# Sparse attention and a split-precision MLP on one core: weights in sixteen 1 MB blocks, and the round trip on ScalarE's queue

## The chip, the cores and the metric

The kernel runs on one core of a Trainium2 chip. A core has TensorE (PE, with its weight load PEld), VectorE (DVE), ScalarE (ACT), GpSimd (POOL) and SyncE (SP), a data memory SBUF of 128 partitions, an accumulation memory PSUM, and 16 DMA engines. The metric is device microseconds for one execution. "Granted clock" is the share of TensorE's full clock that it was given.

## The reference

```python
# q, k, v: (8, 8, 576, 64); x: (8, 576, 512)
scores = q @ k.T / 8                      # heads 0-3: causal, the last 32 positions
scores = where(mask, scores, -1e9)        # heads 4-7: causal, same position modulo 32
attn_out = softmax(scores) @ v            # heads side by side: x
h = (x.T @ U @ V).T                       # rank 32, over the sequence
u = x + h
out = u + max(u @ w_ch1, 0) @ w_ch2       # w_ch1 (512, 2048), w_ch2 (2048, 512)
```

q, k and v are float32. U, V and the two weights are float64: each number reaches the chip as a 64-bit word and is made into a float32 there.

## The kernel before, in words

**The GEMM.** The 8 x 576 rows of u are 36 tiles of 128 rows, 18 blocks of two. Each block n goes through 16 steps (n, fc). A step has a first GEMM (`gemm1`, L521: 12 matmuls of 128x256 into PSUM tile `ph`, for 128 of the 2048 hidden columns), then on ScalarE `gh` (relu, rounded to the short format fp32r, L525) and on VectorE `gl` (the rest that the rounding lost, L526), and two steps later a second GEMM (`gemm2`, L538: 6 matmuls of 128x512 into `acc`). Three matmuls per product give float32 accuracy: `uh`, `ul` and the two halves of a weight tile `w` are the rounded part and the rest. `ph` has two buffers, so the first GEMM of a step waits for gl of two steps earlier. Blocks 0 and 1 run interleaved (32 steps, block 1 two fc behind), then 2 to 17 in order.

**The weights.** 32 chunks of 128x512: four of w1 and four of w2 for every four steps. Each is loaded as 64-bit words (`raw`, 512 KB, L138, issued on SP behind the last other transfer traced) and converted by `to_f32`: ScalarE takes the absolute value of the high word (L104), a clamp at 2^-15 runs on GpSimd, for every third chunk on VectorE (L105), and VectorE makes the exponent, the sign and the low bits (L107, L109, L111). ScalarE rounds it into `w` (L150), GpSimd subtracts to get the rest (L151). The tile being made is `cv`, one of six buffers of tag "att" that the attention shares.

**Attention.** `attention_pair` and `local_pairs` do two heads: scores on TensorE (L215, L221) into `px`, maximum and subtraction on VectorE (L230, L231), exp on ScalarE, transposes (L241), outputs (L253), and the norm on VectorE (L263 to L265, six operations, result `o_sb` or `xg`). Batches 0 and 1 do all eight heads this way; heads 4 to 7 come out in another row order, so their result is written to DRAM (`od`) and read back into `xg` and `xt`: the round trip, L199 to L208, on SP's queue like every transfer. Batches 2 to 7 do those heads on GpSimd and VectorE (`strided_heads`).

**Mix.** `mix_t` (L373, L377; sums `ta`, then `tst`) and `mix_u` (L399, L401) add h. `transposes` (L486) turns u and splits it into `uh` (L490) and `ul` (L491).

**Order.** The program is written as generators that hand out the attention, the conversions and the loads step by step; `convert` and `load_ahead` say how many by when. Batch 0's attention, its mix and the first split come before the first GEMM, batch 1's attention goes between the first 32 steps. A scheduler then sets each engine's order, and an engine runs its list strictly in it. Pair buffers (`qkv`) are three: batch 0's fourth pair waits for the first to be done.

Of the kernel before, what the change touches and what calls it, by code (L numbers as in the profile page):

```python
# [39 lines left out]
def fused_kernel(ctx, tc, pairs, strided, U, V, w1_in, w2_in, masks, eye, out):  # L40
# [57 lines left out]
    def to_f32(raw, p, n, eng=nc.vector):  # L98

        rv = raw.bitcast(I32).rearrange("p (n two) -> p n two", two=2)  # L100
        lo_w, hi_w = rv[:, 0:n, 0], rv[:, 0:n, 1]
# [2 lines left out]
        nc.scalar.activation(out=f, in_=hi_w.bitcast(F32), func=AF.Abs)  # L104
        eng.tensor_scalar(out=f, in0=f, scalar1=TINY, scalar2=None, op0=ALU.max)  # L105
# [1 line left out]
        nc.vector.tensor_scalar(out=i, in0=i, scalar1=3, scalar2=0x3FFFFFF8,  # L107
                                op0=ALU.logical_shift_left, op1=ALU.bitwise_and)
        nc.vector.scalar_tensor_tensor(out=i, in0=hi_w, scalar=-0x40000000, in1=i,  # L109
# [31 lines left out]
    def weights():
        for n, (i, g, t) in enumerate(chunks):
            while wl["n"] <= n:
                next(wl["gen"])
                wl["n"] += 1
# [561 lines left out]
```

## Time and profile before

| | us |
|---|---|
| median of three runs | 1013.37 (1013.08 to 1013.67) |
| profiled execution | 1013.35 |
| its span | 1011.6 |
| PE busy | 940.6 (93%) |
| DVE busy | 608.2 (60%) |
| POOL busy | 391.3 (39%) |
| ACT busy | 267.0 (26%) |
| mean granted clock | 0.96 |

What lies outside the span (1.75 us) is start and end of the execution. Busy time is summed over the whole span, and the early part differs from the rest, so a stretch has to be looked at by itself. PE's ends are modelled: its price for a step is read from the starts of matmuls that follow each other. DMA issues are rows of SPq; the time to landing counts from the issue.

### The profile page before, as it was taken

Reading aid. Unit: us, or ns where it says so; the run is one execution under the profiler, and the core shown is the slowest. Engines: PE = TensorE matmul, PEld = TensorE weight load, DVE = VectorE, ACT = ScalarE, POOL = GpSimd, SP = SyncE. Lnnn points to the kernel's source line nnn. Section 1 sums busy time; section 2 is a strip of 40 time slices with the busy share of each in tenths; the row PEclk is TensorE's granted clock in tenths of the full one; section 3 lists DMA queues with packets and bytes.
Section 4 is the critical chain, followed back from the end, with each engine's and each line's share of the span. In section 5 each row is a group of like instructions: output and inputs, shape, how many; then the busy total and the mean of one; then the engine's idle time right before and its main releaser. Section 6 shows DMA issues by size and latency. Waiting matters only on the chain.

```text
span 1011.6 us, 20383 instructions
## 1 busy us (share of the span) xinstructions
PE 940.6 (93%) x8524; PEld 809.6 (80%) x8524; DVE 608.2 (60%) x1115; ACT 267.0 (26%) x616; POOL 391.3 (39%) x388
## 2 busy tenths in 40 slices
PE   3324999999999999999999999999999999999997
PEld 2213888888888888898888888888888889999996
DVE  4759958886974667514698368847884753212121
ACT  3334433124212421112421142114211421111110
POOL 0647536963951456302385047515661400000000
PEclk8556999999999999999999999999999999999999
DMA  9990141022111221101211121111211001101000
GB/s 358 409 300 1 62 130 48 3 85 96 69 45 42 85 80 45 42 1 43 96 68 45 43 95 70 46 43 58 106 46 43 1 22 22 42 1 43 1 21 21
DMA packets 41037, 72.74 MB, mean 72 GB/s; under 512 B 6224, under 2 KB 25552, under 8 KB 40176
## 3 DMA queue, kind: packets, MB, share of 16 engines
q1 hardware_dynamic: 40944, 71.43, 21.5%
q8 instruction: 67, 1.10, 0.5%
q14 instruction: 26, 0.21, 0.1%
HBM read 52.92 MB, written 10.62 MB: 63 GB/s over the span
## 4 chain that ended last, share of the span: by engine, by line
PE 87%; DVE 7%; DMA 3%; issue 1%; POOL 1%; ACT 0%; SPq 0%; DVEq 0%; ACTq 0%; POOLq 0%
PE ph L521 41%; PE acc L538 38%; DVE cv L109 2%; PE px L538 2%; PE px L221 2%; DVE cv L111 1%; PE px L253 1%; DVE cv L107 1%; PE px L241 1%; DMA xg<-in_U_dram 1%; PE px L373 1%; DMA xg<-od 1%; DMA od<-o_sb 1%; PE px L399 1%; POOL cv L105 0%
## 5 line engine op out<-in xcount | busy, mean ns | idle before, releaser
L521 PE MATMUL ph<-uh,w 128*128 128x256 f32 x2304 | 470.4, 287 | 4.8 <-DVE gl L526 4.1
L521 PEld LDWEIGHTS ph<-uh,w 128*128 128x128 f32 x2304 | 375.5, 189 | 21.2 <-DVE gl L526 4.2
L538 PE MATMUL acc<-w,gh 128*128 128x512 f32 x1088 | 348.0, 399 | 0.0
L521 PE MATMUL ph<-ul,w 128*128 128x256 f32 x1152 | 326.2, 283 | 3.2 <-DVE ul L491 3.2
L526 DVE SCALAR_TENSOR_TENSOR gl<-ph,gh 128x256 fp32r<-128x256 f32 x288 | 121.6, 422 | 291.2 <-ACT gh L525 289.8
L525 ACT ACTIVATE gh<-ph 128x256 fp32r<-128x256 f32 x288 | 110.5, 384 | 518.3 <-PE ph L521 480.8
L335 POOL TENSOR_TENSOR tmp<-st,s_st 128x448 f32<-128x448 f32 (+7 forms) x162 | 137.7, 878 | 276.6 <-DVE st L337 212.0
L521 PEld LDWEIGHTS ph<-ul,w 128*128 128x128 f32 x1152 | 218.4, 190 | 13.6 <-DVE ul L491 3.6
L538 PEld LDWEIGHTS acc<-w,gh 128*128 128x128 f32 x1088 | 193.1, 188 | 32.4 <-issue 0.2
L538 PE MATMUL acc<-w,gl 128*128 128x512 f32 x544 | 215.8, 397 | 0.0
L307 POOL TENSOR_TENSOR tmp<-st 128x576 f32<-128x576 f32 (+6 forms) x162 | 169.4, 1087 | 44.5 <-DVE st L337 34.3
L337 DVE TENSOR_REDUCE st<-tmp 128x64 f32<-128x64 f32 (+8 forms) x162 | 135.3, 874 | 2.8 <-POOL tmp L335 2.5
L538 PEld LDWEIGHTS acc<-w,gl 128*128 128x128 f32 x544 | 102.3, 188 | 20.9
L309 DVE TENSOR_REDUCE s_st<-tmp 128x9 f32<-128x576 f32 (+6 forms) x162 | 86.7, 564 | 5.2 <-POOL tmp L307 5.0
L151 POOL TENSOR_TENSOR w<-cv,w 128x512 fp32r<-128x512 f32 x32 | 46.7, 1468 | 44.7 <-ACT w L150 44.3
L105 POOL TENSOR_SCALAR cv<-cv 128x512 f32<-128x512 f32 x22 | 36.0, 1645 | 45.9 <-ACT cv L104 45.9
L352 ACT COPY xg<-st 32x256 f32<-32x256 f32 x96 | 38.8, 404 | 16.9 <-DVE st L337 14.8
L221 PEld LDWEIGHTS px<-qkv 64*32 64x32 f32 x1440 | 19.7, 112 | 19.8 <-issue 14.6
L508 DVE TENSOR_TENSOR ul<-u,uh 128x1024 fp32r<-128x1024 f32 x15 | 19.0, 1269 | 24.5 <-ACT uh L507 24.5
L221 PE MATMUL px<-qkv 64*32 64x64 f32 (+1 forms) x1440 | 29.5, 236 | 3.5 <-DMA qkv<-in_pairs_dram 2.0
L150 ACT CAST w<-cv 128x512 fp32r<-128x512 f32 x32 | 19.9, 621 | 45.0 <-DVE cv L111 38.3
L384 DVE TENSOR_TENSOR ta<-px,ta 32x256 f32<-32x256 f32 x42 | 17.6, 420 | 21.5 <-ACT ta L382 20.4
(90 smaller groups left out, 559.7 us busy)
## 6 DMA issues: line engine op xcount, KB each, us to landing
raw<-in_w_dram SPq DMA_DIRECT2D x32, 512.0 KB, 10.3
qkv<-in_pairs_dram SPq DMA_DIRECT2D x20, 585.0 KB, 5.5
qkv<-in_pairs_dram SPq DMA_DIRECT2D x20, 576.0 KB, 4.0
out_dram<-xg SPq DMA_DIRECT2D x32, 256.0 KB, 2.1
u<-bt SPq DMA_DIRECT2D x240, 32.0 KB, 1.9
st<-in_strided_dram SPq DMA_DIRECT2D x6, 1152.0 KB, 6.4
st<-in_strided_dram SPq DMA_DIRECT2D x6, 576.0 KB, 4.0
od<-o_sb SPq DMA_DIRECT2D x4, 256.0 KB, 7.1
```

What stands on the lines that cost most here:

```text
L105: eng.tensor_scalar(out=f, in0=f, scalar1=TINY, scalar2=None, op0=ALU.max)
L151: nc.gpsimd.tensor_tensor(out=lo, in0=f, in1=hi.bitcast(F32), op=ALU.subtract)
L221: nc.tensor.matmul(sp[32 * c4:32 * c4 + 32, hh, x0:64 * t + 64], qT[rows, 32 * c:32 * c + 32], kT[rows, k0:32 * c + 32], start=False, stop ...
L307: nc.gpsimd.tensor_tensor(out=tmp[:, 0:n], in0=sk[:, j0:j0 + n], in1=sq[:, i:i + 1].broadcast_to([128, n, D]), op=ALU.mult)
L309: late.append(lambda tmp=tmp, n=n, i=i, j0=j0: nc.vector.tensor_reduce(out=s_st[:, i, j0:j0 + n], in_=tmp[:, 0:n], axis=AX.X, op=ALU.add))
L335: nc.gpsimd.tensor_tensor(out=tv, in0=sv[:, 0:i + 1, d0:d0 + step], in1=s_st[:, i, 0:i + 1].broadcast_to([128, i + 1, step]), op=ALU.mult)
L337: late.append(lambda tv=tv, i=i, d0=d0, step=step: nc.vector.tensor_reduce(out=o_st[:, i, d0:d0 + step], in_=tv.rearrange("p j d -> p d j" ...
L352: nc.scalar.copy(out=xg[32 * i4:32 * i4 + 32, :, cs], in_=o_st[rows, i4:16:4, :])
L521: nc.tensor.matmul(ph[:, 0:W], w_parts[0, g, dc][:, part, fs], ut[:, :, :, dc, :], start=(dc == 0 and i == 0), stop=(dc == NDC - 1 and i = ...
L525: nc.scalar.activation(out=gh[:, 0:W], in_=ph[:, 0:W], func=AF.Relu)
L526: nc.vector.scalar_tensor_tensor(out=gl[:, 0:W], in0=ph[:, 0:W], scalar=0.0, in1=gh[:, 0:W].bitcast(F32), op0=ALU.max, op1=ALU.subtract)
L538: nc.tensor.matmul(accs[n][:, s, :], gt[:, cs], w_parts[1, g, f][:, part, :], start=(fc == 0 and i == 0), stop=(fc == NFC - 1 and i == 2))
```

## The change

**Weights in blocks.** On the host w1 and w2 are laid out as 16 blocks of 128 rows by 1024 words (1 MB): block fc holds what step fc needs of both. Three blocks load freely. Block fc from 3 on is held by a one-column GpSimd copy (L144) that reads block fc - 3's finished tile, so it loads when that conversion is over.

**Conversion.** There is no clamp: ScalarE copies the high word times 2^-112 (L115), VectorE shifts (L117) and puts in sign and low bits (L118, L120), for every half block. The scratch is `cv` (two buffers of its own) and `spare`, parts of the tiles of the last blocks' weights, which also hold batch 0's fourth pair and its attention's temporaries (`ring`); so the fourth pair loads at once, and "att" has four buffers. The first four blocks are converted during batch 0's attention; each later one is queued, on ScalarE and VectorE, behind the first split of u (`marks["split0"]`).

**Round trip.** All transfers from `o_sb` to `od` and back are issued by ScalarE (L97) and not by SP.

```diff
+    def od_dma(out, in_):
+        nc.scalar.dma_start(out=out, in_=in_)
...
-        nc.scalar.activation(out=f, in_=hi_w.bitcast(F32), func=AF.Abs)
-        eng.tensor_scalar(out=f, in0=f, scalar1=TINY, scalar2=None, op0=ALU.max)
+        nc.scalar.activation(out=f, in_=hi_w.bitcast(F32), func=AF.Copy, scale=2.0 ** -112)
...
-        nc.vector.tensor_scalar(out=i, in0=i, scalar1=3, scalar2=0x3FFFFFF8,
-                                op0=ALU.logical_shift_left, op1=ALU.bitwise_and)
-        nc.vector.scalar_tensor_tensor(out=i, in0=hi_w, scalar=-0x40000000, in1=i,
+        nc.vector.tensor_scalar(out=i, in0=i, scalar1=3, scalar2=None, op0=ALU.logical_shift_left)
+        nc.vector.scalar_tensor_tensor(out=i, in0=hi_w, scalar=-0x80000000, in1=i,
...
+        for fc in range(NFC):
+            raw = raws[fc] = const.tile([128, 1024], I64, name=f"w{fc}", tag=f"w{fc}")
+            if fc >= AHEAD:
+                done = w_parts[fc - AHEAD].bitcast(F32)
+                nc.gpsimd.tensor_copy(out=raw.bitcast(F32)[:, 0:1], in_=done[:, 1, 1, 0:1])
+            nc.sync.dma_start(out=raw, in_=w_in[128 * fc:128 * fc + 128, :])
             yield
 
     def weights():
+        for fc in range(NFC):
+            load_ahead(fc + 1)
+            fs = []
+            for i in range(2):
+                early = i and fc < NFC - AHEAD - 2
+                cv = late_part[fc % 2][:, 1536:2048] if early else ap_.tile([128, 512], F32, name="cv", tag="cv", bufs=2)
+                behind = [marks[k][2] for k in ("less", "exp")] if fc < PRE else marks["split0"]
+                with tc.issue_after(behind[0]), tc.issue_after(behind[1]):
+                    fs.append(to_f32(raws[fc][:, 512 * i:512 * i + 512], cv, 128, 512))
+                if not i:
+                    yield
+            parts = w_parts[fc] = const.tile([128, 2, 2, 512], F32R, name=f"w{fc}", tag=f"w{fc}")
+            for i in range(2):
+                nc.scalar.copy(out=parts[:, i, 0], in_=fs[i])
+                nc.gpsimd.tensor_tensor(out=parts[:, i, 1], in0=fs[i], in1=parts[:, i, 0].bitcast(F32), op=ALU.subtract)
+            load_ahead(fc + 1 + AHEAD)
+            yield
...
-        dma(out=od[0:512, oc:oc + 2 * D].rearrange("(t p) d -> p t d", p=128), in_=o_sb[:, 0:4, :])
-        dma(out=od[512:576, oc:oc + 2 * D], in_=o_sb[0:64, 4, :])
+        od_dma(out=od[0:512, oc:oc + 2 * D].rearrange("(t p) d -> p t d", p=128), in_=o_sb[:, 0:4, :])
+        od_dma(out=od[512:576, oc:oc + 2 * D], in_=o_sb[0:64, 4, :])
...
-        return len(chunks) if item[0] >= NLEAD else 8 * (item[1] // FPG) + 4 + item[1] % FPG
+        return 2 * NFC if item[0] >= NLEAD else 2 * item[1] + 2
```

The rows below are the engines' lists; numbers in names tell buffers apart. First, SP's list before, at batch 0's round trip (od, then xg and xt):

```order
L138 DMA raw0_2_2_474<-in_w1_dram 128x512
L138 DMA raw0_2_3_476<-in_w1_dram 128x512
L88 DMA qkv_882<-in_pairs_dram 128x1152
L88 DMA qkv_882<-in_pairs_dram 128x1170
L88 DMA od_84<-o_sb_465 128x4x128
L88 DMA od_84<-o_sb_465 64x128
L88 DMA qkv_962<-in_pairs_dram 128x1152
L88 DMA qkv_962<-in_pairs_dram 128x1170
L88 DMA qkv_1137<-in_pairs_dram 128x1152
L88 DMA qkv_1137<-in_pairs_dram 128x1170
L88 DMA xg_480<-od_84 32x4x256 x4
L88 DMA xt_481<-od_84 32x256 x2
```

The same place now, on ScalarE's list (w3 is block 3, ring_85 the o_sb of the second class pair, PT copies of the attention are L264):

```order
L115 ACTIVATE cv_589<-w3_414 128x512
L115 ACTIVATE spare_103<-w3_414 128x512
L97 DMA od_84<-ring_85 128x4x128
L97 DMA od_84<-ring_85 64x128
L264 COPY ring_86<-px_471 128x576
L162 CAST w3_606<-cv_589 128x512
L162 CAST w3_606<-spare_103 128x512
L97 DMA xg_426<-od_84 32x4x256 x4
L97 DMA xt_427<-od_84 32x256 x2
```

The trip left SP's list, where weights and batch 1's pairs stood ahead of it, and now stands on ScalarE between the steps of block 3's conversion. Second, VectorE before, in the first GEMM steps (about 120 to 127 us; six gl stand ahead of these rows):

```order
L526 SCALAR_TENSOR_TENSOR gl_1208<-ph_1194,gh_1207 128x256
L109 SCALAR_TENSOR_TENSOR cv_1126<-raw1_2_2_553,cv_1126 128x512
L107 TENSOR_SCALAR cv_1211<-cv_1211 128x512
L111 SCALAR_TENSOR_TENSOR cv_1126<-raw1_2_2_553,cv_1126 128x512
L230 TENSOR_REDUCE mx_1258<-px_1148 128x10
L109 SCALAR_TENSOR_TENSOR cv_1211<-raw1_2_3_555,cv_1211 128x512
L231 TENSOR_TENSOR s_sb_1257<-px_1148,mx_1258 128x2x5x64
L111 SCALAR_TENSOR_TENSOR cv_1211<-raw1_2_3_555,cv_1211 128x512
L526 SCALAR_TENSOR_TENSOR gl_1302<-ph_1288,gh_1301 128x256
L526 SCALAR_TENSOR_TENSOR gl_1430<-ph_1416,gh_1429 128x256
```

And VectorE now, at the end of its conversions (w15 is the last block; gl_1696, gl_1727 and gl_1766 are those of the 17th, 18th and 19th step):

```order
L551 SCALAR_TENSOR_TENSOR gl_1696<-ph_1682,gh_1695 128x256
L117 TENSOR_SCALAR cv_1699<-cv_1699 128x512
L551 SCALAR_TENSOR_TENSOR gl_1727<-ph_1713,gh_1726 128x256
L118 SCALAR_TENSOR_TENSOR cv_1699<-w15_1539,cv_1699 128x512
L117 TENSOR_SCALAR cv_1730<-cv_1730 128x512
L120 SCALAR_TENSOR_TENSOR cv_1699<-w15_1539,cv_1699 128x512
L283 TENSOR_SCALAR rt_1394<-px_1357 128x2x4
L118 SCALAR_TENSOR_TENSOR cv_1730<-w15_1539,cv_1730 128x512
L284 RECIPROCAL rt_1394<-rt_1394 128x2x4
L120 SCALAR_TENSOR_TENSOR cv_1730<-w15_1539,cv_1730 128x512
L285 TENSOR_TENSOR xg_1140<-px_1357,rt_1394 128x2x4x64
L283 TENSOR_SCALAR rt_1394<-px_1357 64x2
```

Before, the conversions thin out after the eighth step's gl and the last stands behind the 22nd; now 24 of the 32 halves stand among the first 18 steps' gl, and none later. (Lines from L97 on are those of the changed kernel: L264 was L244, L283 to L285 the norm, L551 gl.)

More of the change, by code (lines that the diff above doesn't have):

```diff
@@ L26 @@
 N_PE_T = 3
-LDM = 4
+AHEAD = 3
+PRE = 4
 CONVM = 1.35
@@ L39, in fused_kernel @@
 @with_exitstack
-def fused_kernel(ctx, tc, pairs, strided, U, V, w1_in, w2_in, masks, eye, out):
+def fused_kernel(ctx, tc, pairs, strided, U, V, w_in, masks, eye, out):
     nc = tc.nc
@@ L120, in small_weights @@
         yield
-        f = to_f32(raw, 128, 5 * R)
-        nc.vector.tensor_copy(out=U_sb.rearrange("p t r -> p (t r)"), in_=f)
+        f = to_f32(raw, att([128, 640], "cu"), 128, 5 * R)
+        nc.scalar.copy(out=U_sb.rearrange("p t r -> p (t r)"), in_=f)
         yield
-        f = to_f32(raw[0:R, 5 * R:5 * R + S], R, S)
+        f = to_f32(raw[0:R, 5 * R:5 * R + S], att([128, 640], "cu"), R, S)
         nc.scalar.copy(out=Vst[0:32], in_=f)
-        nc.scalar.copy(out=Vst[32:64], in_=f)
+        nc.scalar.copy(out=Vst[32:64], in_=Vst[0:32].bitcast(F32))
@@ L139, in load_weights @@
             yield
     def weights():
[L142 to L145, printed above, removed]
-            f = to_f32(raws[i, g, t], 128, 512, nc.vector if n % 3 == 2 else nc.gpsimd)
-            parts = const.tile([128, 2, 512], F32R, name=f"w{i}_{g}_{t}", tag=f"w{i}_{g}_{t}")
-            w_parts[i, g, t] = parts
-            hi, lo = parts[:, 0], parts[:, 1]
-            nc.scalar.copy(out=hi, in_=f)
-            nc.gpsimd.tensor_tensor(out=lo, in0=f, in1=hi.bitcast(F32), op=ALU.subtract)
+        for fc in range(NFC):
[14 more added lines that the diff above has]
+            load_ahead(fc + 1 + AHEAD)
@@ L152, in weights @@
             yield
+    late_part = []
     wl = {"gen": load_weights(), "n": 0}
     def load_ahead(n):
-        while wl["n"] < min(n, len(chunks)):
+        while wl["n"] < min(n, NFC):
             next(wl["gen"])
@@ L404, in mix_u @@
                 yield from transposes(t // 2)
+                marks.setdefault("split0", marks["split"])
         pv = psx1()
@@ L429, in first_attention @@
         pairs0 = early_pairs(b, ORDER0)
+        spare = [const.tile([128, 2048], F32, name="ring", tag=f"w{fc}") for fc in (NFC - 3, NFC - 4)]
+        ring.extend(s[:, 640 * k:640 * k + 640] for k in range(3) for s in spare)
         next(pairs0[0])
@@ L489, in transposes @@
                 hi, lo = (u[:, s].rearrange("p a d x -> p d a x") for u in (uh, ul))
-                nc.scalar.copy(out=hi, in_=src)
-                nc.vector.tensor_tensor(out=lo, in0=src, in1=hi.bitcast(F32), op=ALU.subtract)
+                first = nc.scalar.copy(out=hi, in_=src)
+                second = nc.vector.tensor_tensor(out=lo, in0=src, in1=hi.bitcast(F32), op=ALU.subtract)
+                marks["split"] = (second.ins, first.ins)
                 yield
@@ L537, in gemm2 @@
             for i, (gt, part) in enumerate(((gh, 0), (gh, 1), (gl, 0))):
[L538 removed]
+                nc.tensor.matmul(accs[n][:, s, :], gt[:, cs], w_parts[fc][:, 1, part, :],
                                  start=(fc == 0 and i == 0), stop=(fc == NFC - 1 and i == 2))
@@ L564, in convert @@
     def convert(n):
-        while counts["conv"] < min(n, len(chunks)):
+        while counts["conv"] < min(n, 2 * NFC):
             next(conv)
```

91 lines of the change are left out of this document (48 added, 43 removed).

## Prediction

> **What bounds the kernel now.** I read the slices of the page first, then busy time by stretch.
>
> ```profile
> PE   3324999999999999999999999999999999999997
> PEclk8556999999999999999999999999999999999999
> GB/s 358 409 300 1 62 130 48 3 85 96 69 45 42 85 80 45 42 1 43 96 68 45 43 95 70 46 43 58 106 46 43 1 22 22 42 1 43 1 21 21
> ```
>
> Each slice is 25.3 us. TensorE is full from the fifth slice to the end; before that it is mostly idle at half clock, while the DMA engines run at about 400 GB/s for three slices and then stop.
>
> ```profile
> 61.20:112.00 50.80, 26.38 (x325) 20.62 (x325) 50.37 (x71) 23.18 (x44) 35.70 (x22) 0.67 0.23 88
> 112.00:1011.60 899.60, 893.80 (x7566) 775.58 (x7564) 526.16 (x980) 226.37 (x545) 337.29 (x351) 1.00 0.17 51
> ```
>
> Columns: length, then PE, PEld, DVE, ACT, POOL busy with counts, clock, DMA share, GB/s. From 112 us on, TensorE sets the pace. From 61 to 112 VectorE does (50.4 of 50.8 us). Before that it is a transfer, as the chain that ended last says, with the first rows of the GEMM from the timeline:
>
> ```profile
> 39.93 8.35 DMA od<-o_sb
> 49.69 8.43 DMA xg<-od
> 58.25 1.94 PE L373 MATMUL ph<-xg,U_sb 128*32 128x256 f32 x16 [18.70 <-DMA xg<-od]
> 88.79 0.58 PE L521 MATMUL ph<-ul,w 128*128 128x256 f32 x1 [3.21 <-DVE ul L491]
> ```
>
> The round trip of batch 0 through DRAM takes 8.35 and 8.43 us because weights and batch 1's pairs stand ahead of it on the one queue. The mix then starts at 58.25, the first full GEMM step at 88.79, and TensorE waits for VectorE's gl again and again until 112 (the idle time in the L521 row below). So the change can only move the first 112 us; after that I need the TensorE work that is left.
>
> ```profile
> 109.07 0.86 PE L241 MATMUL px<-ident,s_sb 128*128 128x128 f32 x5 [0.48 <-ACT s_sb L234]
> 111.98 0.39 PE L521 MATMUL ph<-uh,w 128*128 128x256 f32 x1
> 119.93 0.28 PE L521 MATMUL ph<-uh,w 128*128 128x256 f32 x1
> 121.37 0.63 PE L538 MATMUL px<-w,gh 128*128 128x512 f32 x2
> 122.77 0.28 PE L521 MATMUL ph<-uh,w 128*128 128x256 f32 x1
> L521 PE MATMUL ph<-uh,w 128*128 128x256 f32 x40 | 10.0, 335 | 4.8 <-DVE gl L526 4.1 <-ACT uh L490 0.7
> L538 PE MATMUL acc<-w,gh 128*128 128x512 f32 x12 | 4.3, 446 | 0.0
> ```
>
> By start times a first GEMM costs 1.44 us, a second 1.40, the attention of one pair 2.91 (109.07 to 111.98). The last two rows (82.4 to 112 us) count what was done by 112: 8 such matmuls make a first GEMM and 4 a second, so 5 and 3 steps of the 288, and about 1.4 of batch 1's four pairs.
>
> **The change, part by part.**
>
> *Loads.* Batch 0's fourth pair now loads ahead of all weights. It came late before:
>
> ```profile
> 29.64 1.31 PE L221 MATMUL px<-qkv 64*32 64x32 f32 x72 [1.65 <-DMA qkv<-in_pairs_dram]
> 15.40 0.71 ACT L104 ACTIVATE cv<-xg 32x576 f32<-32x576 f32 x1 [0.39 <-DMA xg<-in_V_dram]
> ```
>
> V, the last transfer ahead of the weights, landed by 15.4. At 400 GB/s the fourth pair (1.19 MB) then lands about 18, blocks 0, 1 and 2 (1.05 MB each) about 21, 23.5 and 26. Only these three are free to load; block 3 waits for block 0's last subtraction on POOL. From block 0's landing VectorE has nine passes on cv and most of a norm ahead of block 0's last pass (about 7 us at the prices below), then come a cast and two subtractions (3): 31. A lone load costs what the transfers between 110 and 140 us cost:
>
> ```profile
> st<-in_strided_dram SPq DMA_DIRECT2D x1, 1152.0 KB, 7.1
> qkv<-in_pairs_dram SPq DMA_DIRECT2D x1, 585.0 KB, 4.8
> xg<-od SPq DMA_DIRECT2D x4, 128.0 KB, 2.7
> ```
>
> 1024 KB lies between 4.8 and 7.1; I take 6, so block 3 lands at 37.3.
>
> *Round trip on ScalarE.* The write of the second class pair (o_sb is ready at 40 by VectorE's order) stands behind block 3's two conversions on ScalarE, a new wait, which ends about 39, just inside. The read-back stands behind block 3's casts, hence behind VectorE's last step on block 3, about 45.5. It no longer waits in SP's queue: its landing costs between 2.7 us (row above) and the old 8.43. I take 2.7, since by the sum above only block 5 is then in flight, and 3.4 us for six issues. The mix has its inputs at 51.6 instead of 58.2. On SP nothing is gained or lost: the queue then only feeds later blocks.
>
> A rule speaks against this part. The Trainium skill (DMA: Bandwidth & Descriptors, Issuing engines are not separate DMA queues) says that transfers issued from several engines run on the same 16 DMA engines and interleave. The trace of before has one queue and can't show it; by that rule alone the trip would keep its 8.4 us each way, which is the third rival below.
>
> *Between mix and GEMM.* Before, VectorE interleaved conversions here; now they are held behind the first split. The chain, by its own rows:
>
> ```profile
> 60.12 0.65 PE L377 MATMUL ph<-xt,U_sb 64*32 64x64 f32 x16
> L384 DVE TENSOR_TENSOR ta<-ph,ta 32x256 f32<-32x256 f32 x6 | 2.5, 420 | 12.0 <-ACT ta L382 11.8
> 68.52 1.19 PE L399 MATMUL px<-tst,Vst 96*128 96x512 f32 x2 [7.75 <-DVE tst L389]
> 74.91 1.11 PE L486 MATMUL px<-ident,xg 128*128 128x128 f32 x4 [3.91 <-DVE xg L401]
> L491 DVE TENSOR_TENSOR ul<-px,uh 128x512 fp32r<-128x512 f32 x4 | 2.7, 678 | 0.0
> L490 ACT CAST uh<-px 128x512 fp32r<-128x512 f32 x4 | 2.3, 585 | 3.8 <-PE px L486 3.8
> ```
>
> After the last mix matmul (about 52): 4.3 us to tst (six additions of 0.42, and at most 0.6 each, by the last row, for a copy ahead and two casts behind), 1.2 for the first two Vst products, 1.7 to the first added x tile and the wait for the last product, four transposes of 1.11, a cast and a split (0.6 + 0.68): 12 us. So the first full GEMM step starts at 64 instead of 88.8, 25 us earlier. What hid the conversions is gone, too: VectorE idles from about 46 to 52 and in this chain, and only 8 of 32 half blocks are converted at 64.
>
> *The conversion in the GEMM.* 24 halves then stand in VectorE's order among the first 18 steps (about 1.35 a step), and gl of each step, which frees the PSUM bank of step + 2, stands behind them.
>
> ```profile
> L109 DVE SCALAR_TENSOR_TENSOR cv<-raw,cv 128x512 int32<-128x512 int32 x14 | 14.2, 1024 | 0.1
> L105 DVE TENSOR_SCALAR cv<-cv 128x512 f32<-128x512 f32 x5 | 3.6, 725 | 0.0
> L526 DVE SCALAR_TENSOR_TENSOR gl<-ph,gh 128x256 fp32r<-128x256 f32 x5 | 2.1, 412 | 0.0
> 61.20:112.00 50.80, 39.21 (x47) 16.85 (x27) 35.70 (x22) 0.67 0.23 88
> 99.03 3.03 POOL L151 TENSOR_TENSOR w<-cv,w 128x512 fp32r<-128x512 f32 x2 [0.41 <-ACT w L150]
> 99.42 1.50 DVE L107 TENSOR_SCALAR cv<-cv 128x512 int32<-128x512 int32 x1
> 129.68 0.43 DVE L107 TENSOR_SCALAR cv<-cv 128x512 int32<-128x512 int32 x1
> 130.15 0.69 DVE L109 SCALAR_TENSOR_TENSOR cv<-raw,cv 128x512 int32<-128x512 int32 x1
> 96.70 1.92 POOL L105 TENSOR_SCALAR cv<-cv 128x512 f32<-128x512 f32 x1
> 97.53 0.76 DVE L111 SCALAR_TENSOR_TENSOR cv<-raw,cv 128x512 int32<-128x512 int32 x1
> ```
>
> The fourth row is VectorE's, ScalarE's and POOL's time on cv alone from 61.2 to 112: 39.2 us for 14 chunks and 5 clamps, so (39.2 - 3.6)/14 = 2.54 a chunk. Alone a chunk is 0.43 + 0.69 + 0.69 = 1.81; the rest is the wait while POOL subtracts (1.50 for 0.43 at 99.42). Beside POOL's clamp at 96.70 there was no such wait (0.76). So removing the clamp, 22 passes on POOL and 10 on VectorE, shortens the chain but leaves VectorE's price a half near 2.54 (bounds 1.81 and 2.54). VectorE from 64: 24 x 2.54 = 61.0; 18 gl of 0.41, 7.4; a split, 0.7; four pairs of scores (0.81 + 0.81) and of norms (1.76), 13.5:
>
> ```profile
> L231 DVE TENSOR_TENSOR s_sb<-px,mx 128x640 f32<-128x640 f32 x1 | 0.8, 811 | 0.0
> 114.21 0.16 DVE L263 TENSOR_SCALAR rt<-px 128x8 f32<-128x8 f32 x1
> 115.69 0.28 DVE L265 TENSOR_TENSOR o_sb<-px,rt 64x128 f32<-64x128 f32 x1
> ```
>
> 82.6, and 3 for ten DMA issues that now sit between ScalarE's gh: 86 us, to 150. TensorE could do the same stretch in 64 (20 x 1.44 + 17 x 1.40 + 4 x 2.91), so it loses 22 of the 25 us it started earlier, but it arrives further along: at 150 it has 20 first and 17 second GEMMs and all four pairs, against 5, 3 and 1.4 at 112 before. That is 15 x 1.44 + 14 x 1.40 + 2.6 x 2.91 = 48.8 us of its 899.6. Fewer temporaries (4 for 6) and the small POOL copies cost nothing: POOL stands idle among its later rows, and block loads are three ahead.
>
> **Sum.** 64 + 86 + (899.6 - 48.8) = 1000.8 us of span; 1.75 lies outside (1013.35 - 1011.6 in the profiled execution, 0.02 under the median): 1002.5 us.
>
> **Rivals.**
> 1. VectorE doesn't gate. At 1.81 a half it needs 65 us, as TensorE: 64 + 65 + 850.8 + 1.75 = 982. For it: the clamp's 15 us on POOL between 61 and 112 are gone. Against: the 1.50 falls in a subtraction, which stays. The Trainium skill (SBUF — State Buffer, Who interferes with whom) says that an operation of VectorE with two inputs in SBUF and one of GpSimd that reads SBUF exclude each other for the whole instruction. The subtractions agree (1.50), the clamp at 96.70 doesn't (0.76); by that page the clamps held VectorE as well, and this rival would come.
> 2. Slower: the load chain. Block n + 3 loads only after block n's subtraction, so blocks 6, 9, 12 and 15 hang in a row. Block 6 ends about 20 us into the GEMM. I price a link at 7 for the load and 13 for copies, two blocks' turn on VectorE, casts and subtractions: 80 us, just inside the 86. It decides from 25.5 us a link (block 15 at 97, the time as before); at 27, with ScalarE's in-order waits in each, 101 us: 1018.
> 3. No change worth measuring: the trip still takes 8.4 each way beside the loads. The write lands 3.4 us after its reader is ready, the read-back costs 5.7 more: 1011.6.
>
> **How the numbers follow.** Forecast 0.57 (own range 993 to 1010), rival 1 0.12, rival 2 0.17, rival 3 0.14. The measurement can tell 0.2%, 2 us. Faster takes the forecast but for 0.03, rival 1 and half of rival 3: 0.73; same 0.09; slower 0.18. The range 986 to 1015 leaves out most of rival 1 below and half of rival 2 above.
>
> **What would show it.** Right: the mix near 50 to 52 us, the first full GEMM step near 64, read-back landing in about 3 us; VectorE full for some 80 us afterwards, gl as releaser of the first GEMM, subtractions beside stretched steps; TensorE full from about 150. Wrong: VectorE idle there (rival 2, with ScalarE or DMA as releaser), TensorE full from 70 (rival 1), the mix at 60 (rival 3).

## The result, and the profile after

The changed kernel takes 998.75 us (median of four runs, 997.99 to 999.63), beside 1013.52 of the kernel before on the same chip: ratio 0.9853, 95% interval 0.9836 to 0.9870. The profiled execution of the changed kernel took 999.63, its span 997.7, so 1.9 us lie outside.

The slices of the page, 24.9 us each, as shown for the kernel before:

```profile
PE   4257999999999999999999999999999999999997
PEclk9999999999999999999999999999999999999999
GB/s 362 281 59 203 242 175 2 86 51 101 41 60 53 62 73 40 33 15 76 49 77 46 36 96 70 46 43 96 71 46 43 2 22 22 43 1 43 1 22 22
```

TensorE is full from the fifth slice on, as before, but the third and the fourth went from 2 and 4 tenths to 5 and 7. The weights no longer come in one burst: they move with their use, up to the sixth slice. Where the start of the GEMM stands is read from the chain of waits (first three rows) and from TensorE's timeline (last two):

```profile
38.96 6.59 DMA od<-ring
45.54 4.64 issue
51.53 5.02 DMA xg<-od
...
56.65 1.93 PE L393 MATMUL ph<-xg,U_sb 128*32 128x256 f32 x16 [14.11 <-DMA xg<-od]
70.51 0.39 PE L546 MATMUL ph<-ul,w 128*128 128x256 f32 x1 [0.22 <-DVE ul L517]
```

The first full GEMM step begins at 70.5 us, 18.3 earlier than before (88.79). Little of that is the round trip: the mix starts at 56.65 instead of 58.25. The stretch from mix to GEMM shrank from 30.5 us to 13.9. Why the trip stayed slow is in the DMA issues between 28 and 62 us (last column: median us from issue to landing):

```profile
w<-in_w_dram SPq DMA_DIRECT2D x4, 1024.0 KB, 7.8
qkv<-in_pairs_dram SPq DMA_DIRECT2D x2, 585.0 KB, 9.4
xg<-od ACTq DMA_DIRECT2D x4, 128.0 KB, 5.3
od<-ring ACTq DMA_DIRECT2D x1, 256.0 KB, 11.6
```

The 256 KB part of the od write, issued at 38.39, landed 11.6 us later (the chain's row of 6.59 ends with ScalarE's last cast of block 3, at 45.54, and the chain calls the rest "issue"), then the read-back took 5.3. Beside the write moved weight blocks 4 and 5 (issued at 35.8 and 41.4) and two pairs of batch 1; beside the read-back only block 6 (issued at 47.9, landed at 55.3).

The stretches around the start and after it (length, PE, PEld, DVE, ACT, POOL, clock, DMA share, GB/s), the last two rows from the first full step to the end, before and after:

```profile
46.00:59.60 13.60, 2.52 (x32) 1.09 (x32) 0.00 (x0) 0.37 (x2) 1.77 (x3) 1.00 0.64 193
70.00:117.00 47.00, 39.82 (x569) 33.24 (x569) 46.47 (x78) 23.92 (x46) 25.00 (x21) 0.96 0.55 197
70.00:100.00 30.00, 23.42 (x344) 19.45 (x344) 29.86 (x50) 16.78 (x33) 14.25 (x13) 0.97 0.49 173
117.00:147.40 30.40, 29.64 (x383) 25.35 (x383) 21.79 (x44) 13.91 (x28) 10.65 (x10) 1.00 0.62 205
147.40:997.70 850.30, 844.02 (x6919) 736.03 (x6917) 486.27 (x904) 204.97 (x504) 312.01 (x332) 1.00 0.15 47
...
88.80:1011.60 922.80, 912.45 (x7865) 791.42 (x7865) 549.32 (x1010) 235.69 (x563) 353.63 (x360) 1.00 0.16 50
70.50:997.70 927.20, 913.19 (x7865) 794.54 (x7865) 554.03 (x1023) 242.30 (x577) 347.66 (x363) 1.00 0.19 60
```

VectorE idles from 46 to 59.6 us, for the trip. From 70 to 117 it is full, and TensorE works 39.8 of these 47 us; nearly all that it loses, it loses before 100 (23.4 of 30 us). From 117 to the last conversion (147.4) TensorE is nearly full and VectorE is not. The last two rows are the balance of the change: 18.3 us earlier, and 4.4 us longer from there to the end (927.2 for 922.8), TensorE idle 14.0 instead of 10.3. 18.3 - 4.4 = 13.9, the difference of the spans.

TensorE's wait has one name. The GEMM's first group between 70 and 150 us (busy, mean ns, idle time ahead and its releaser), then POOL, VectorE and TensorE in one place of the timeline:

```profile
L546 PE MATMUL ph<-uh,w 128*128 128x256 f32 x162 | 35.0, 297 | 7.3 <-DVE gl L551 7.2
...
86.92 1.54 POOL L163 TENSOR_TENSOR w<-cv,w 128x512 fp32r<-128x512 f32 x1 [3.11 <-ACT w L162]
88.42 1.74 POOL L163 TENSOR_TENSOR w<-spare,w 128x512 fp32r<-128x512 f32 x1
87.23 1.79 DVE L120 SCALAR_TENSOR_TENSOR cv<-w,cv 128x512 int32<-128x512 int32 x1
88.94 1.77 DVE L118 SCALAR_TENSOR_TENSOR spare<-w,spare 128x512 int32<-128x512 int32 x1
90.63 0.41 DVE L551 SCALAR_TENSOR_TENSOR gl<-ph,gh 128x256 fp32r<-128x256 f32 x1
91.09 0.39 PE L546 MATMUL ph<-uh,w 128*128 128x256 f32 x1 [1.57 <-DVE gl L551]
```

Two steps of VectorE that take 0.69 alone take 1.79 and 1.77 beside POOL's two subtractions. In VectorE's order gl of the GEMM step stands behind them, and TensorE waits for gl.

### The profile page after: what moved, and what is told of

Read it like the earlier page. It is cut to its first block, busy times and chain, and to the rows that moved or that the text cites. A ratio compares the mean times of both kernels' runs of the same rounds, so it can differ in the third digit from the quotient of the medians.

```text
span 997.7 us, 20318 instructions
## 1 busy us (share of the span) xinstructions
PE 940.9 (94%) x8524; PEld 812.8 (81%) x8524; DVE 594.0 (60%) x1102; ACT 265.3 (27%) x617; POOL 360.2 (36%) x379
## 4 chain that ended last, share of the span: by engine, by line
PE 85%; DVE 8%; DMA 3%; issue 2%; ACT 1%; ACTq 0%; POOL 0%; SPq 0%; DVEq 0%
PE ph L546 40%; PE acc L562 37%; PE px L240 2%; DVE cv L120 1%; DVE cv L118 1%; PE px L562 1%; PE px L273 1%; DMA xg<-in_V_dram 1%; PE px L393 1%; PE px L419 1%; PE px L261 1%; DVE spare L118 1%; DMA od<-ring 1%; DVE cv L117 1%; DVE spare L117 1%
## 5 line engine op out<-in xcount | busy, mean ns | idle before, releaser
L546 PEld LDWEIGHTS ph<-uh,w 128*128 128x128 f32 x2304 | 378.6, 190 | 24.9 <-DVE gl L551 9.7
L562 PE MATMUL acc<-w,gh 128*128 128x512 f32 x1088 | 341.8, 394 | 0.0
L546 PE MATMUL ph<-ul,w 128*128 128x256 f32 x1152 | 330.8, 287 | 0.2 <-DVE ul L517 0.2
L551 DVE SCALAR_TENSOR_TENSOR gl<-ph,gh 128x256 fp32r<-128x256 f32 x288 | 121.4, 422 | 276.1 <-ACT gh L550 274.9
L327 POOL TENSOR_TENSOR tmp<-st 128x576 f32<-128x576 f32 (+6 forms) x162 | 168.5, 1072 | 27.5 <-DVE s_st L329 21.1
L357 DVE TENSOR_REDUCE st<-tmp 128x64 f32<-128x64 f32 (+8 forms) x162 | 137.4, 875 | 8.1 <-POOL tmp L355 7.4
L329 DVE TENSOR_REDUCE s_st<-tmp 128x9 f32<-128x576 f32 (+6 forms) x162 | 89.0, 566 | 12.1 <-POOL tmp L327 11.4
L163 POOL TENSOR_TENSOR w<-cv,w 128x512 fp32r<-128x512 f32 x21 | 28.4, 1364 | 99.0 <-ACT w L162 94.6
L240 PE MATMUL px<-qkv 64*32 64x64 f32 (+1 forms) x1368 | 31.8, 237 | 0.6 <-issue 0.6
L421 DVE TENSOR_TENSOR xg<-px,xg 128x512 f32<-128x512 f32 x30 | 19.5, 682 | 8.7 <-PE px L419 8.7
L569 DVE TENSOR_TENSOR xg<-acc,xg 128x512 f32<-128x512 f32 x30 | 19.5, 685 | 7.5 <-PE acc L562 7.4
```

Of the source, the lines that this page charges most:

```text
L163: nc.gpsimd.tensor_tensor(out=parts[:, i, 1], in0=fs[i], in1=parts[:, i, 0].bitcast(F32), op=ALU.subtract)
L240: nc.tensor.matmul(sp[32 * c4:32 * c4 + 32, hh, x0:64 * t + 64], qT[rows, 32 * c:32 * c + 32], kT[rows, k0:32 * c + 32], start=False, stop ...
L327: nc.gpsimd.tensor_tensor(out=tmp[:, 0:n], in0=sk[:, j0:j0 + n], in1=sq[:, i:i + 1].broadcast_to([128, n, D]), op=ALU.mult)
L329: late.append(lambda tmp=tmp, n=n, i=i, j0=j0: nc.vector.tensor_reduce(out=s_st[:, i, j0:j0 + n], in_=tmp[:, 0:n], axis=AX.X, op=ALU.add))
L357: late.append(lambda tv=tv, i=i, d0=d0, step=step: nc.vector.tensor_reduce(out=o_st[:, i, d0:d0 + step], in_=tv.rearrange("p j d -> p d j" ...
L546: nc.tensor.matmul(ph[:, 0:W], w_parts[fc][:, 0, part, 128 * dc:128 * dc + 128], ut[:, :, :, dc, :], start=(dc == 0 and i == 0), stop=(dc ...
```

## The experiments

Each timed kernel ran beside the kernel before; the ratio's interval is given. To compare them, each has its first full step (TensorE's timeline), the span from there to the end, and how long TensorE was idle in it (stretches like the last two rows above):

| kernel | time us | ratio to before | first full step | from there to the end | TensorE idle in it |
|---|---|---|---|---|---|
| before | 1013.5 | 1 | 88.8 | 922.8 | 10.3 |
| changed | 998.75 | 0.9836 to 0.9870 | 70.5 | 927.2 | 14.0 |
| 1 trip on SyncE | 995.06 | 0.9808 to 0.9835 | 69.1 | 924.7 | 10.8 |
| 2 clamp back | 997.52 | 0.9833 to 0.9860 | 66.3 | 929.5 | 14.4 |
| 3 not held | 1007.81 | 0.9938 to 0.9965 | 85.4 | 920.5 | 8.6 |
| 4 two more early | 1002.48 | 0.9882 to 0.9909 | 72.0 | 927.8 | 13.1 |
| 5 loads behind trip | 996.31 | 0.9810 to 0.9840 | 63.1 | 931.0 | 15.8 |
| 6 pace by number | 998.42 | 0.9832 to 0.9866 | 69.4 | 926.8 | 12.9 |
| 7 one input on POOL | 991.50 | 0.9764 to 0.9793 | 67.0 | 922.6 | 10.1 |
| 8 before, trip on ScalarE | 1029.88 | 1.0140 to 1.0171 | 101.8 | 925.9 | 11.8 |
| 9 one half a step | 998.25 | 0.9843 to 0.9870 | 70.1 | 926.1 | 11.2 |
| 10 = 5 and 9 | 990.77 | 0.9764 to 0.9790 | 63.3 | 926.1 | 11.0 |
| 11 = 10, trip on SyncE | 987.74 | 0.9728 to 0.9754 | 63.2 | 923.3 | 8.9 |
| 12 = 10, pace 1.15 | 985.95 | 0.9714 to 0.9741 | 64.4 | 920.5 | 8.6 |

The last three columns come from one profiled execution each. Kernel 6 runs VectorE's steps from 70 to 150 us in the order of the changed kernel and so serves as its repeat: it starts 1.1 us earlier and idles 1.1 less, and differences of that size are not told apart. What is not idle in the stretch is TensorE's busy time, 912 to 915 us, and the granted clock has a part in it. In the traces the clock is 0.50 for some time after the first full step: 3.4 us in the changed kernel (98.2 to 101.6), 10.2 in experiment 5 (69.9 to 73.3 and 86.9 to 93.7), 8.6 in experiment 9 (the first 1.8 us, and 3.4 from 153.9 and from 174.3), 6.0 in 10 (the first 2.6, and 3.4 from 158.1), 2.7 in 11 and 1.6 in 12.

**1. The round trip back on SyncE's queue.**

```diff
     def od_dma(out, in_):
-        nc.scalar.dma_start(out=out, in_=in_)
+        nc.sync.dma_start(out=out, in_=in_)
```

> The changed kernel with the round trip of od issued on SyncE's queue again, all else as changed. In the changed kernel the larger od write landed 11.6 us after its issue and the four xg transfers 5.3 us after theirs, while the DMA engines moved 300 to 400 GB/s of weights and pairs. Theory A (the queue is what a transfer waits in, the recorded sum's step): the trip gets 8 to 10 us longer, the mix begins near 66 us and the time is 1007 to 1010. Theory B (the engines' load sets the landing, on either queue): the mix begins at 55 to 59 us as it did (56.65), the time is 997 to 1001.

995.06, a little faster than on ScalarE's queue; its interval lies just below that of the changed kernel. The issues between 28 and 62 us, and the first full step:

```profile
xg<-od SPq DMA_DIRECT2D x4, 128.0 KB, 6.6
od<-ring SPq DMA_DIRECT2D x1, 256.0 KB, 6.4
...
69.06 0.58 PE L546 MATMUL ph<-ul,w 128*128 128x256 f32 x1
```

The write landed in 6.4 instead of 11.6, the read-back in 6.6 instead of 5.3, and the mix began at 54.73. Theory A, that the trip waits in SyncE's queue, is out; Theory B has the mechanism, though the time lies 2 us below its range. Moving the trip to ScalarE's queue bought nothing, and the change is 3.7 us slower with it. The 1.5 us by which the GEMM starts earlier here are hardly more than the spread between the changed kernel and kernel 6; experiment 11 shows where else the time can lie. The DMA engines moved as much from 38 to 50 us in both (351 and 345 GB/s). What differs is the order: on SyncE's queue the second pair is issued behind the large part of the write (38.85 and 40.13) and not ahead of it (36.24).

**2. The clamp back.**

```diff
-        nc.scalar.activation(..., func=AF.Copy, scale=2.0 ** -112)
+        nc.scalar.activation(..., func=AF.Abs, scale=2.0 ** -112)
+        eng.tensor_scalar(out=f, in0=f, scalar1=0.0, scalar2=None, op0=ALU.max)   # POOL, each third on VectorE
```

> The changed kernel with a maximum put back between ScalarE's copy and VectorE's shift in each conversion (a maximum with 0 after an absolute value, so the results stay as they are), two of three on POOL and one of three on VectorE as in the kernel before. Between 70 and 117 us VectorE is full in the changed kernel (46.1 of 46.6 us) and converts 16 halves at 2.41. Theory A (POOL's clamp leaves VectorE alone; only the five on VectorE cost, 0.42 each): 1000 to 1003, the halves on VectorE stay near 2.4 besides the clamps. Theory B (a clamp on POOL holds VectorE as a subtraction does; ten of them, 0.7 to 1 us each): 1007 to 1012, halves near 3.2. If VectorE did not set the pace there: 998 to 1000.

997.52, with an interval that overlaps the changed kernel's, and below both theories: removing the clamp is worth nothing that could be measured. But the edit moved more than the clamp. The clamps delay the first conversions, so the loads of blocks 3 to 6 come later (block 3 at 38.9 instead of 31.7) and the od write, issued at 34.8, lands in 5.5 us; the first full step moves to 66.3. From there on the kernel is 2.3 us slower (929.5 for 927.2). How much of that is Theory A's price for the clamps isn't shown, since in experiment 5 an earlier start alone made this stretch longer. Beside POOL's clamp VectorE's two-input steps are stretched little:

```profile
92.64 1.92 POOL L116 TENSOR_SCALAR cv<-cv 128x512 f32<-128x512 f32 x1
92.13 1.08 DVE L121 SCALAR_TENSOR_TENSOR cv<-w,cv 128x512 int32<-128x512 int32 x1
93.47 0.76 DVE L121 SCALAR_TENSOR_TENSOR spare<-w,spare 128x512 int32<-128x512 int32 x1
```

The first of the two began beside a subtraction, which ended at 92.67; the second ran inside the clamp and took 0.76. Of 15 such steps beside clamps alone the longest took 1.09.

**3. Conversions not held behind the split.**

```diff
-                behind = [marks[k][2] for k in ("less", "exp")] if fc < PRE else marks["split0"]
+                behind = [marks[k][2] for k in ("less", "exp")]
```

> The changed kernel without the order that puts the conversions of blocks 4 and later behind the first split; they stand in VectorE's order as early as their program order allows: three blocks in its idle 46 to 59.6 us, two more between the mix and the split. Theory A (holding them is what starts the GEMM early): the first full step begins at 80 to 89 us instead of 70.5 and the time is 1004 to 1008. Theory B (what counts is VectorE's whole work up to 117 us, wherever it stands; with the idle 13.7 us filled, TensorE never waits later): the start moves to 78 to 85, TensorE is full from there on, 992 to 1000.

1007.81, Theory A: 9.1 us of the change's 14.8 come from this one order. In VectorE's timeline the conversions now stand between the mix's steps again, and the first full step waits for the split:

```profile
64.66 2.34 DVE L404 TENSOR_TENSOR ta<-ph,ta 32x256 f32<-32x256 f32 x6
66.92 1.45 DVE L117 TENSOR_SCALAR cv<-cv 128x512 int32<-128x512 int32 x1
...
85.41 0.58 PE L546 MATMUL ph<-ul,w 128*128 128x256 f32 x1 [2.31 <-DVE ul L517]
```

The start falls back by 14.9 us; 6.7 come back afterwards (920.5 for 927.2), since more blocks are ready. So Theory B holds in part, but not for the sum. The other 5.7 us of the change (blocks, the fourth pair's early load, the shorter conversion) were not taken apart by a run; by experiment 1 the trip's queue is no part of them.

**4. Six early blocks instead of four.**

```diff
-PRE = 4
+PRE = 6
```

> The changed kernel with blocks 4 and 5 too converted ahead of the mix (six early blocks instead of four), where VectorE stands idle from 45.9 to 59.6 us for the round trip. Four halves at 2.41 us leave the full stretch of VectorE. Theory A (VectorE's conversions hold TensorE from 70 to 117 us, where it lost about 12 us): the full step still begins near 70.5, TensorE loses 2 to 4 us in place of 12, the time is 988 to 991. Theory B (TensorE is held there by something else, the wait of each block for its load and POOL): 996 to 1000. If the conversions delay the mix instead: the mix at 60 or later and 1000 to 1004.

1002.48, slower: the third case by its time, though the mix's matmuls were not late (55.48). With two blocks less in the GEMM, TensorE's wait for gl fell only from 7.2 us to 5.1, and the start came 1.5 us later, since ScalarE's and VectorE's work on block 5 stood ahead of the mix's additions. That work was late by the trip: block 5 had landed at 49.3, but on ScalarE its conversion stood behind the read-back's six issues (49.6 to 52.9), which waited for the write, and began at 54.0:

```profile
60.66 1.54 DVE L404 TENSOR_TENSOR ta<-ph,ta 32x256 f32<-32x256 f32 x4 [1.52 <-ACT ta L402]
...
L546 PE MATMUL ph<-uh,w 128*128 128x256 f32 x160 | 35.4, 302 | 5.1 <-DVE gl L551 5.1
```

The number of halves left is thus not what gates alone; how many stand ahead of one gl may be.

**5. Loads of blocks 4 to 6 behind the read-back.**

```diff
+                if fc in (PRE, PRE + 1, PRE + 2):   # the copy ahead of the load reads the landed x tile
+                    nc.gpsimd.tensor_copy(out=raw.bitcast(F32)[:, 0:1], in_=xgs[0][:, 0, 256:257])
...
-            load_ahead(fc + 1)
+            load_ahead(fc + 1 if fc < PRE else fc + AHEAD)
...
-            load_ahead(fc + 1 + AHEAD)
+            load_ahead(fc + 1 + AHEAD if fc >= PRE else PRE)
```

> The changed kernel, trip on ScalarE's queue, with the loads of blocks 4, 5 and 6 issued only when the read-back of od has landed (the small POOL copy ahead of each load reads the landed x tile instead of block 1's to 3's low part). In the changed kernel these three blocks and two pairs moved while the larger od write took 11.6 us and xg 5.3. Theory A (what a landing costs is the load on the engines): the write lands in 4 to 7 us, the read-back in 2.5 to 4, the mix begins at 48 to 52 and the first full step at 62 to 66 in place of 70.5; the end comes 4 to 8 us earlier, 991 to 995, less if blocks 7 to 9 then come late. Theory B (the small transfers cost that by themselves): the write still 10 to 12 us, the mix at 55 to 58, 997 to 1001.

The trip did what Theory A said, on ScalarE's queue as in the changed kernel (issues between 28 and 64 us, TensorE's timeline):

```profile
xg<-od ACTq DMA_DIRECT2D x4, 128.0 KB, 2.7
od<-ring ACTq DMA_DIRECT2D x1, 256.0 KB, 6.6
...
49.28 1.94 PE L396 MATMUL ph<-xg,U_sb 128*32 128x256 f32 x16 [6.88 <-DMA xg<-od]
63.15 0.39 PE L549 MATMUL ph<-ul,w 128*128 128x256 f32 x1 [0.21 <-DVE ul L520]
```

Between 38 and 50 us the engines moved 196 GB/s instead of 345. But of 7.4 us at the start only about 2.4 reached the end (996.31): the stretch after it became 3.8 us longer. Half of that is idle time (15.8 for 14.0): an earlier GEMM alone runs into VectorE again. The other half is busy time (915.2 for 913.2), in stretches at a lower clock; where the changed kernel had 1.00, 1.00 and 0.91, this one had 0.84, 0.85 and 0.81:

```profile
70.00:80.00 10.00, 9.92 (x93) 8.36 (x91) 9.79 (x14) 4.27 (x9) 7.49 (x6) 0.84 0.36 115
80.00:90.00 10.00, 7.21 (x175) 6.17 (x176) 9.93 (x14) 5.22 (x12) 7.34 (x6) 0.85 0.57 205
90.00:100.00 10.00, 8.10 (x41) 6.77 (x41) 10.00 (x21) 6.15 (x11) 4.26 (x4) 0.81 0.87 293
```

So what is in flight sets the landings, and not the whole of an earlier start reaches the end.

**6. A slower pace, by number.** `CONVM = 1.35` became `1.0`.

> The changed kernel with one half block converted for each GEMM step instead of 1.35 (the need two steps ahead still goes first). From the first step to the end of the conversions one step is about 2.84 us of TensorE and, with its share of the four pairs, 3.3; VectorE at 1.35 x 2.41 + 0.41 + 0.5 has 4.2, at 1.0 it has 3.3. In the changed kernel TensorE then lost about 12 us to gl, which stands behind the conversions in VectorE's order; with two blocks converted early (the fourth experiment) it lost as much. Theory A (the pace of conversions per step, not their sum, is what gates): TensorE loses 3 to 6 us, the time is 990 to 995. Theory B (the sum of VectorE's work gates, wherever it stands): 997 to 1001. If blocks come too late at that pace: above 1001.

998.42, no change, and no test: on VectorE blocks 4 to 10 are converted in the same order as before, so the number that asks for conversions doesn't set where they stand. Experiment 9 sets it by an explicit order.

**7. One input on POOL.**

```diff
-                nc.gpsimd.tensor_tensor(out=parts[:, i, 1], in0=fs[i], in1=parts[:, i, 0].bitcast(F32), op=ALU.subtract)
+                nc.gpsimd.tensor_scalar(out=parts[:, i, 1], in0=fs[i], scalar1=2.0 ** -12, scalar2=None, op0=ALU.mult)
```

> The changed kernel with POOL's subtraction (two inputs) replaced by a multiplication of one input of the same size, so the low halves of the weights are not computed. VectorE's steps beside a subtraction took 1.4 to 1.8 us instead of 0.42 to 0.69, some 10 us over the 16 halves between 70 and 117. Theory A (what stretches them is POOL's two-input operation): halves at 1.8 to 2.0 us, TensorE loses 4 to 7 us in place of 12, 991 to 995. Theory B (any POOL operation on SBUF stretches them, or the stretch is not what gates): halves at 2.3 to 2.5, 997 to 1001.

991.50, Theory A. POOL's instruction is as long as before (mostly 1.5 to 1.6 us), yet VectorE's steps beside it are hardly stretched:

```profile
77.41 1.59 POOL L163 TENSOR_SCALAR w<-spare 128x512 fp32r<-128x512 f32 x1
77.91 0.76 DVE L120 SCALAR_TENSOR_TENSOR cv<-w,cv 128x512 int32<-128x512 int32 x1
78.59 0.68 DVE L118 SCALAR_TENSOR_TENSOR spare<-w,spare 128x512 int32<-128x512 int32 x1
```

TensorE idles 10.1 us after the start instead of 14.0, and the start itself comes 3.5 earlier. So the stretch comes from POOL's two-input operation, and without it this kernel is about 7 us faster, the earlier start included. The Trainium skill (SBUF — State Buffer, Who interferes with whom) lets a VectorE operation with two SBUF inputs contend with any GpSimd operation that reads SBUF. This trace agrees only for POOL operations with two inputs: 25 two-input steps of VectorE ran beside POOL's one-input operation in 0.64 to 0.98 us, 0.70 in the mean, and alone they take 0.68.

**8. The kernel before with its trip on ScalarE's queue.** As experiment 1, in the other direction and in the kernel before.

> The kernel before with one part of the change alone: the round trip of od issued on ScalarE's queue. Before, the write landed in 8.35 us and the read-back in 8.43, on SyncE's queue among weight loads at 400 GB/s. Theory A (as with the trip put back on SyncE's queue: the load on the engines sets it, and the own queue is no quicker): the mix begins at 57 to 62 us instead of 58.25 and the time is 1011 to 1016. Theory B (the recorded sum's: on its own queue the read-back lands in about 3 us): the mix at 50 to 53, 1004 to 1009.

1029.88, 16 us slower, outside both theories. The edit moved more than the trip. With the od transfers gone from SyncE's queue 22 weight loads followed each other, and three pairs' loads came behind them; and the od write, whose tile VectorE had finished at 35.5, was issued on ScalarE only at 53.92, ahead of a cast (SyncE's queue, ScalarE's queue and ScalarE):

```profile
21.93 28.41 SPq L141 DMA_DIRECT2D raw<-in_w_dram  x22
51.35 9.54 SPq L88 DMA_DIRECT2D qkv<-in_pairs_dram  x6
53.92 1.74 ACTq L99 DMA_DIRECT2D od<-o_sb  x2
55.75 0.62 ACT L153 CAST w<-cv 128x512 fp32r<-128x512 f32 x1 [21.20 <-DMA raw<-in_w_dram]
```

In the trace that issue waits for a completion semaphore on which a weight load, issued by SyncE at 43.62, landed at 53.84. ScalarE, which runs its list in order, stood from 34.6 until then, and the cast and the attention's copy behind the issue with it. So this doesn't price the queue alone; it shows what an issue costs that waits for an unrelated load on an engine with other work.

**9. One half for each GEMM step, by order.**

```diff
-                behind = ... if fc < PRE else marks["split0"]
+                behind = ... if fc < PRE else marks.get("step", marks["split0"])   # gl and gh of the latest step
...
-CONVM = 1.35
+CONVM = 1.0
```

> The changed kernel with every half block of blocks 4 to 15 ordered behind gl of the latest GEMM step, one half for a step, so that VectorE's order has a gl after each half. (The sixth experiment asked for the same pace by number alone and left the order of blocks 4 to 10 as it was, so it did not try this.) In the changed kernel up to three halves stood ahead of one gl, and TensorE waited 7.2 us for gl between 70 and 150. Theory A (how many halves stand ahead of a gl is what gates): TensorE loses 3 to 7 us after the first full step in place of 12, the time is 991 to 995. Theory B (the sum of VectorE's work gates, wherever it stands): 997 to 1001. If blocks are converted too late at that pace: 1001 to 1006, with TensorE waiting for w instead of gl.

998.25, by its time Theory B; by the trace both. Between 70 and 150 us TensorE waits for gl no more: the group that idled 7.3 us there idles 0.0, and at 150 TensorE is 3.75 first and 3.2 second GEMMs further than in the changed kernel, about 10 us of work. But the conversions now last until 173 us, beside batch 1's mix, and there most of it is lost again: TensorE idles 5.4 us between 150 and 190, where the changed kernel idles 0.0, and its clock is 0.91 instead of 1.00 (TensorE's group, VectorE's timeline, then a stretch):

```profile
L546 PE MATMUL ph<-uh,w 128*128 128x256 f32 x191 | 40.0, 291 | 0.0
171.80 1.21 DVE L120 SCALAR_TENSOR_TENSOR cv<-w,cv 128x512 int32<-128x512 int32 x1
150.00:190.00 40.00, 34.61 (x190) 29.90 (x189) 34.16 (x61) 9.07 (x21) 31.85 (x29) 0.91 0.06 18
```

Order gates within the stretch, and what was deferred meets the next stage.

**10. Late loads and one half a step together.** The edits of 5 and 9.

> The fifth experiment (loads of blocks 4 to 6 behind the read-back, first full step at 63.15, 996.31) and the ninth (one half for a step) together. Theory A (the two losses are separate): the sum of the two gains on the changed kernel, the first full step near 63 and 986 to 991. Theory B (with an earlier start VectorE's sum of conversions sets the end of the stretch): 994 to 998, VectorE full to about 110.

990.77, Theory A's time, but not by its sum: the parts alone gave 2.4 and 0.5 us, together they gave 8. With the start at 63.3 the conversions end at 162 instead of 173, and between 150 and 190 TensorE idles 2.8 us instead of 5.4. A further part may be the clock: 5 had 6.8 us more at 0.50 after its start than the changed kernel, 9 had 5.2 more, and both together only 2.6. If half of such time is lost, that is 4.7 of the 5 us by which the whole exceeds the sum (3.8 with kernel 6 in place of the changed kernel). This is an estimate from the traces; no run tested it, and the cause stays open.

**11. The same with the trip on SyncE's queue.** The edit of experiment 1 on 10.

> The tenth experiment (990.77: late loads and one half for a step) with the round trip on SyncE's queue instead of ScalarE's. The trip now shares the engines with two pairs only, no weights; on ScalarE's queue the write landed in 6.5 us and the read-back in 2.7 there. Theory A (the load on the engines sets the landings, and the queue only through what is ahead in it): the same mix, near 49, and 989 to 992. Theory B (ScalarE's queue has a worth of its own once the weights are gone): a write of 8 to 9 us, the mix at 51 to 54, 993 to 997.

987.74, better than either theory. The first trip is the same (mix at 48.89), so ScalarE's queue gives it nothing even without weights beside it. What differs is batch 1's trip. As in the changed kernel, in experiment 10 its six issues stood on ScalarE between GEMM steps, gh and so gl behind them, and TensorE waited (ScalarE's queue, ScalarE, TensorE):

```profile
105.64 1.89 ACTq L97 DMA_DIRECT2D xg<-od  x4
107.56 1.01 ACTq L97 DMA_DIRECT2D xt<-od  x2
108.62 0.38 ACT L553 ACTIVATE gh<-ph 128x256 fp32r<-128x256 f32 x1 [4.08 <-PE ph L549]
109.52 0.38 PE L549 MATMUL ph<-uh,w 128*128 128x256 f32 x1 [0.39 <-DVE gl L554]
```

In experiment 11 its waits for gl between 70 and 150 are 0.7 us instead of 2.0, and TensorE worked 49.2 of the 50 us from 100 to 150, in experiment 10 47.8. That is about half of the 3 us; another 1.1 lies between 150 and 190, where the conversions end 2.5 us earlier.

**12. 1.15 halves for each step.** Experiment 10 with `CONVM = 1.15`.

> The tenth experiment with 1.15 halves for a step instead of 1.0. In it TensorE lost 2.2 us between 100 and 150 and 2.8 between 150 and 170 us, where VectorE (18 of 20 us) has the last conversions beside later work. Theory A (the conversions end too late at one a step): they end some 8 us earlier, the loss after 150 goes, 987 to 990. Theory B (what is gained there is lost ahead, at gl): 990 to 993.

985.95, the lowest median, though its interval overlaps that of experiment 11: 27.5 us under the kernel before (0.9728) and 12.8 under the change. The conversions end at 148 instead of 162, the loss after 150 is nearly gone, and no wait for gl came in its place:

```profile
64.40:984.90 920.50, 911.92 (x7866) 793.91 (x7865) 555.24 (x1023) 242.52 (x578) 348.41 (x363) 1.00 0.19 62
```

The trip is still on ScalarE's queue there; 11 and 12 together were not run.

## Why the prediction was right, and where it was not

The forecast was 1002.5; 998.75 came, with the sign and the mechanism as forecast: an earlier GEMM start, then conversions on VectorE ahead of gl. That the time came so close is partly luck: it rests on two terms that were off in opposite directions.

- **Round trip (mix inputs at 51.6).** Failed. They came at 56.55, and the step that failed is the write, to which the sum gave no time of its own. ScalarE had finished block 3's casts at 45.54, where 45.5 was forecast, but the write, issued at 38.39 beside blocks 4 and 5 and two pairs, landed only at 50.0 and held the read-back for 4.6 of the 5 us. The read-back itself was mis-sized too: one block was in flight, as the sum had it (block 6 and not 5), and it took 5.3, not the 2.7 of a transfer with little beside it; but the path has four issues in it, not six, and that made up for it. With those loads moved away (5) the read-back took the 2.7 that I had taken, the mix began at 49.3 and the first step at 63.15, where 64 was forecast. My reading of the trip before, slow because of what stood ahead of it in one queue, fell with experiment 1. The rule that I set against my own value (the Trainium skill, DMA: Bandwidth & Descriptors, Issuing engines are not separate DMA queues) was right, and experiments 1 and 11 show it: the same trip is no quicker on ScalarE's own queue (mix at 48.94 in experiment 10, 48.89 in 11).
- **Mix to GEMM, 12 us.** Held: last mix matmul to first full step took 11.4 (59.1 to 70.5), and experiment 3 shows that the order behind the split makes it. (The terms as I wrote them add up to 12.9, not 12.)
- **S = 64.** Came as 70.5, by the first term alone.
- **D = 86 us, VectorE the pace.** Too long: the last conversion ended at 147.4, 77 us after the start. A half cost 2.41 (16 halves between 70.4 and 117, 38.6 us of VectorE on the tiles cv and spare), not 2.54, and the last eight 2.0, since few subtractions ran beside them. VectorE was full for 47 us, not for 80; TensorE was nearly full from 100, not from 150.
- **TensorE work left at that point.** Held: 20.25 first and 18 second GEMMs and four pairs were done at 150 (20, 17 and 4 forecast), and 847.7 us were left there (850.8 forecast); 850.3 were left at 147.4, where the conversions ended.
- **The sum.** S was 6.4 late, D 9 short: the terms cancel to 2.6 of span, the work left takes off another 0.5, and the 1.9 outside against 1.75 add little. 70.4 + 77 + 850.3 = 997.7.
- **"Loses 22 of the 25 us".** Wrong in kind. TensorE idled 14.0 us after the start, and 10.3 before the change; only 4.4 of 18.3 went back. I had compared a gated stretch with a free one, not with the gated one that it replaced.
- **Rival 1, VectorE doesn't gate.** Did not come: a half cost 2.41 and then 2.0, not 1.81, and TensorE waited for gl. The clamp held VectorE little, as I had read it (2 and 7), and no gain from its removal could be measured. The 1.50 that I counted for two inputs is a shift with one; the two-input steps beside subtractions are the 1.79 and 1.77 above.
- **Rival 2, the load chain.** Did not come as priced: VectorE was full to 117, while ScalarE waited 5.5 us for weights between 70 and 117. After 117 its sign shows in part: VectorE idled 6.0 us until 147.4 for ScalarE's copies, but these waited 4.1 us for POOL's subtractions and never for a load, and TensorE lost only 0.8 there.
- **Rival 3, the trip stays at 8.4 each way.** Came for the trip's length (11.6 and 5.3), but only in half for its delay: the mix stood at 56.65, between my 51.6 and the 60.7 that this rival gives. Its time stayed away because D was 9 us short, which I hadn't foreseen.

## What to carry to other kernels

Moving a small transfer to another engine's queue doesn't take it out of the load: look at what is in flight at its issue, hold those transfers back, and price the issues on the engine that now makes them, with all that these issues wait for. When work is moved off an idle stretch into a full one, order it so that little stands ahead of the result that the bottleneck waits for, and see where its tail ends: in these runs a pace of one half a step met the next stage, and 1.35 the present one. And compare the new stretch with the stretch that it replaces, not with an ideal one.
